# Sparse attention and a feed-forward layer on one core: value-row copies ahead of the weight loads, PSUM banks split by engine, plain bf16 transposes

## The chip, the cores and the metric

One core of a Trainium2 chip. In this kernel TensorE makes the matrix products, into buffers in the memory called PSUM (which is divided into banks); ScalarE, VectorE and GpSimd copy, reduce and cast, for the most part to and from the memory called SBUF; SyncE, and GpSimd for the weights, issue the transfers (DMA). A tile is a buffer that the kernel names. A timeline line gives start, length, engine and instruction, and in brackets how long the engine was idle before it and what ended that wait.

The metric is the time of one execution on the device, in microseconds (us). One profiled execution of each kernel gives the trace; its span is some 1.7 to 2.2 us shorter than the time. One of the four timed executions of the kernel before took 266.46 us and is left out of ratios as slow.

## The reference

Four batches, eight heads, 768 positions, head dimension 64. A query attends to the keys within 15 positions and to one maximum of keys (with the mean of values) for each block of 32. The result goes through a feed-forward layer.

```python
k_sum = k.reshape(B, H, nb, 32, D).max(axis=3)
v_sum = v.reshape(B, H, nb, 32, D).mean(axis=3)
scores = concat([where(|i - j| < 16, scale * q @ k.T, -1e9),
                 scale * q @ k_sum.T + log(32)])
attn = softmax(scores) @ concat([v, v_sum])
x = attn.transpose(0, 2, 1, 3).reshape(3072, 512)
h = x @ w_in                       # 512 -> 2048
out = (h * sigmoid(1.702 * h)) @ w_out   # 2048 -> 512
```

## The kernel before

The work goes in eight half units u0 to u7 of 384 tokens, two for each batch. A half unit is a first layer (16 tiles of four matmuls "ph") and a second layer (48 matmuls "po"). The attention of the next half unit is laid between the matmuls of the second layer. In the first layer of every odd half unit, the next batch's k and q are transposed on TensorE; I call this the preparation.

Tensors that the argument needs: kx holds transposed keys, with halo columns of the neighbours and 24 block maxima (ks) in every tile of 128 columns. qz holds transposed queries of two heads, with zeros in the half that belongs to the other head. vw holds values by tile; after v is cast into it, four copies move halo rows inside vw ("vw<-vw") and two copies bring in the block sums ("vw<-vs"); the function vrows casts the block sums (vs) on VectorE and has SyncE issue these six row copies. Only then can the first value product ("ps_av") run.

Keys are transposed by a product with the identity into an f32 PSUM tile of two banks. One engine copies them out, then VectorE takes maxima and halos:

```python
def tk_own(p, s, own):
    big = psb.tile([128, 1024], F32, name="ps_k", tag="big")
    for half in range(2):                       # one bank each
        p3 = big[:, half * 512:half * 512 + HALF].rearrange("p (c r) -> p r c", r=JH)
        for r in range(JH):
            pe.matmul(out=p3[:, r], lhsT=..., rhs=ident, start=True, stop=True)
    copy(own, at(flat, 0, ...), at(big, 0, ...))            # both banks at once
    return big

def tk_rest(p, s, big):
    dve.tensor_reduce(out=ks..., in_=at(big, 0, ...), axis=AX.X, op=ALU.max)
    ...                                         # three halo copies out of PSUM, one copy of ks
```

The start of the program, cut:

```python
for p in range(NP):
    clear_kx(dve, p, 0)
clear_vw(dve, 0)
dve.memset(vs[:, :, D:VC], float(block))
for p in range(NP):
    clear_qz(dve, p, 0)          # eight zeroings, while VectorE has no data yet
warmth(8)
...                              # k and v of batch 0: casts, tk_own, tk_rest, vsum
cast_q(dve, 0, 0)
cast_q(pool, 1, 0)
vrows(0)                         # vs cast on VectorE, six row copies issued by SyncE
for p in range(NP):
    load_q(0, p, 1)
tq(0, 0, act, dve, True)
...
cast_q(pool, 3, 0)
load_w_in(0)                     # weights at once; w_in 1..3 and w_out after the attention
scores(0, 0, 0)
...
```

The softmax here doesn't subtract the row's maximum and nothing guards it: scores larger than these inputs give would overflow.

Of the kernel before, what the change touches and what calls it, by code (L numbers as in the profile page):

```python
# [34 lines left out]
def kernel(  # L35
# [17 lines left out]
    QT = 64  # L53
# [18 lines left out]
    castp = ctx.enter_context(tc.tile_pool(name="cast", bufs=3))  # L72
# [10 lines left out]
    def load_k(b, p):  # L83
        t = stage.tile([128, 2, 2, JH, D], F32, name=f"kf{p}", tag=f"kf{p}")
        for half in range(2):
            sp.dma_start(out=t[:, half].rearrange("p h r d -> p h (r d)"),
                         in_=k[b, 2 * p:2 * p + 2, half * HALF:(half + 1) * HALF]
                         .rearrange("h (p r) d -> p h (r d)", r=JH))
        raw["k", p] = t

    def load_q(b, p, half):
        t = stage.tile([128, 2, JH, D], F32, name=f"qf{p}{half}", tag=f"qf{p}{half}")
        sp.dma_start(out=t.rearrange("p h r d -> p h (r d)"),
                     in_=q[b, 2 * p:2 * p + 2, half * HALF:(half + 1) * HALF]
                     .rearrange("h (p r) d -> p h (r d)", r=JH))
        raw["q", p, half] = t
# [39 lines left out]
    dve.memset(mk, 1.0)  # L136
# [13 lines left out]
    def finish_masks():  # L150
# [4 lines left out]
        for par, halo in ((0, 96), (1, 32)):  # L155
# [10 lines left out]
    qz = [[keep.tile([128, TH, 2, QT], BF16, name=f"qz{p}_{s}") for s in range(2)]  # L166
          for p in range(NP)]
# [14 lines left out]
    def clear_qz(eng, p, s):  # L182
        eng.memset(qz[p][s][0:64, :, 1, :], 0.0)
        eng.memset(qz[p][s][64:128, :, 0, :], 0.0)
# [24 lines left out]
    def cast_k(eng, p, eng2=None):  # L209
        t = castp.tile([128, 2, JH, 2, D], BF16, name="kb", tag="kb")  # L210
        for half in range(2):
            copy((eng2 or eng) if half else eng, t[:, half].rearrange("p r h d -> p h r d"), raw["k", p][:, half])
        cast["k", p] = t

    def cast_q(eng, p, half):
        t = castp.tile([128, JH, 2, D], BF16, name="qb", tag="qb")
        copy(eng, t.rearrange("p r h d -> p h r d"), raw["q", p, half])
        cast["q", p] = t
# [40 lines left out]
    def tk(p, s, own=dve):  # L259
        tk_rest(p, s, tk_own(p, s, own))  # L260

    def tk_own(p, s, own):
        src = cast.pop(("k", p))
        big = psb.tile([128, 1024], F32, name="ps_k", tag="big")
        for half in range(2):
            p3 = big[:, half * 512:half * 512 + HALF].rearrange("p (c r) -> p r c", r=JH)
            for r in range(JH):
                pe.matmul(out=p3[:, r], lhsT=src[:, half, r].rearrange("p h d -> p (h d)"),
                          rhs=ident, start=True, stop=True)

        flat = kx[p][s].rearrange("p t c -> p (t c)")
        copy(own, at(flat, 0, [[768, 2], [256, JH], [192, 2], [1, 64]]),
             at(big, 0, [[512, 2], [128, JH], [64, 2], [1, 64]]))
        return big

    def tk_rest(p, s, big):
        flat = kx[p][s].rearrange("p t c -> p (t c)")
        ks = attp.tile([128, nb], BF16, name="ks", tag="ks")
        dve.tensor_reduce(out=ks.rearrange("p (h n) -> p h n", h=2),
                          in_=at(big, 0, [[512, 2], [block, nb // 2], [1, block]]),  # L280
                          axis=AX.X, op=ALU.max)

        dve.tensor_copy(out=at(flat, 256 + 96, [[768, 2], [256, 2], [-176, 2], [1, 16]]),
                        in_=at(big, 128 - 16, [[512, 2], [128, 2], [16, 2], [1, 16]]))
        dve.tensor_copy(out=at(flat, 768 + 96, [[-176, 2], [1, 16]]),
                        in_=at(big, HALF - 16, [[512 - HALF + 16, 2], [1, 16]]))
        dve.tensor_copy(out=at(flat, 128 + 32, [[768, 2], [256, JH], [-48, 2], [1, 16]]),
                        in_=at(big, 64 - 16, [[512, 2], [128, JH], [16, 2], [1, 16]]))
        dve.tensor_copy(out=at(flat, 64, [[256, NJ], [64, 2], [1, nb]]),
                        in_=ks.unsqueeze(1).unsqueeze(1).to_broadcast([128, NJ, 2, nb]))  # L290

    def tq(p, half, e0, e1, early=False):
        src = cast.pop(("q", p))
        big = (pmm.tile([128, 512], F32, name="ps_q1", tag="mm") if early else
               psb.tile([128, 1024], F32, name="ps_q", tag="big"))
        ps = big[:, 0:HALF]
        p3 = ps.rearrange("p (c r) -> p r c", r=JH)
        for r in range(JH):
            pe.matmul(out=p3[:, r], lhsT=src[:, r].rearrange("p h d -> p (h d)"),
                      rhs=ident, start=True, stop=True)  # L300
        for hh, eng in ((0, e0), (1, e1)):
            r = slice(hh * 64, hh * 64 + 64)
            copy(eng, qz[p][half][r, :, hh, :], ps[r].rearrange("p (t c) -> p t c", c=QT))
# [3 lines left out]
    def scores(b, half, p):  # L307
        a_sb[p] = attp.tile([128, 2, TH, QT], BF16, name="a_sb", tag="a_sb")
        a = a_sb[p]
        big = psb.tile([128, 1024], F32, name="ps_s", tag="big")  # L310
        ps = big[:, 0:2 * HALF].rearrange("p (t h c) -> p t h c", h=2, c=QT)
        for i in range(TH):
            pe.matmul(out=ps[:, i].rearrange("p h c -> p (h c)"),
                      lhsT=kx[p][b % 2][:, half * TH + i, :],
                      rhs=qz[p][half][:, i].rearrange("p h c -> p (h c)"),
                      start=True, stop=True)
        act.activation(out=a.rearrange("p h t c -> p t h c"), in_=ps,
                       func=ACT.Exp, scale=scale)
        af = a.rearrange("p h t c -> p h (t c)")
        dve.tensor_mul(af, af, mk[:, half * TH:(half + 1) * TH, :]  # L320
                       .rearrange("p t c -> p (t c)").unsqueeze(1)
                       .to_broadcast([128, 2, TH * QT]))
# [64 lines left out]
    for p in range(NP):  # L387
        clear_qz(dve, p, 0)
    warmth(8)

    cast_k(act, 0, dve)
    big0 = tk_own(0, 0, act)
    cast_k(act, 1, dve)
    tk_rest(0, 0, big0)
    big1 = tk_own(1, 0, act)
    cast_k(pool, 2)
    tk_rest(1, 0, big1)
    cast_k(pool, 3)
    warmth(2)
    cast_v(act, 0, 0, 1)  # L400
    cast_v(pool, 0, 0, 0)
    big2 = tk_own(2, 0, act)
    vsum(0, (0,))
    cast_v(act, 0, 1, 1)
    cast_v(pool, 0, 1, 0)
    tk_rest(2, 0, big2)
    vsum(0, (1,))
    big3 = tk_own(3, 0, act)
    for j in (2, 3, 4, 5):
        cast_v(act, 0, j, 1)  # L410
        cast_v(pool, 0, j, 0)
        if j == 2:
            tk_rest(3, 0, big3)
            finish_masks()
        warmth(1)
        vsum(0, (j,))
    cast_q(dve, 0, 0)
    cast_q(pool, 1, 0)
    vrows(0)
    for p in range(NP):  # L420
        load_q(0, p, 1)
    tq(0, 0, act, dve, True)
    cast_q(dve, 2, 0)
    tq(1, 0, act, dve, True)
    cast_q(pool, 3, 0)
    load_w_in(0)
    scores(0, 0, 0)
    tq(2, 0, act, dve, True)
    scores(0, 0, 1)
    tq(3, 0, act, dve, True)  # L430
    scores(0, 0, 2)
    warmth(1)
    values(0, 0, 0)
    scores(0, 0, 3)
    warmth(1)
# [11 lines left out]
    for c in range(1, 4):  # L447
        load_w_in(c)
# [21 lines left out]
    for u in range(2 * B):  # L470
        b, half = u // 2, u % 2
        todo = {}
        if half == 0:

            for p in range(NP):
                cast_q(pool, p, 1)
                todo[3 + 3 * p] = [lambda p=p: tq(p, 1, dve, dve)]
                if p == 2:
                    todo[3 + 3 * p].append(lambda: None)
        elif b + 1 < B:  # L480
            s = (b + 1) % 2
            todo = {1: [lambda: tk(0, s)], 2: [lambda: tk(1, s)],
                    4: [lambda: vsum(s, (0, 1, 2))],
                    5: [lambda: vsum(s, (3, 4, 5)), lambda: vrows(s)],
                    6: [lambda: tk(2, s)], 8: [lambda: tk(3, s)],
                    9: [lambda: tq(0, 0, dve, dve)], 11: [lambda: tq(1, 0, dve, dve)],
                    12: [lambda: tq(2, 0, dve, dve)], 14: [lambda: tq(3, 0, dve, dve)]}
            cast_k(pool, 0)
            cast_k(pool, 1)
            for j in range(NJ):  # L490
                cast_v(pool, s, j, 0)
                cast_v(pool, s, j, 1)
            cast_k(pool, 2)
            cast_q(pool, 0, 0)
        for nt in range(NT):
            ff_in(u, nt)
            if half == 1 and b + 1 < B:
                if nt == 2:
                    cast_k(pool, 3)
                if nt == 9:  # L500
                    cast_q(pool, 1, 0)
                    cast_q(pool, 2, 0)
                if nt == 11:
                    cast_q(pool, 3, 0)
            for f in todo.get(nt, ()):
                f()
        if half == 0 and b + 1 < B:
            pass
# [4 lines left out]
        for ms, part in order:  # L513
# [4 lines left out]
            if half == 0 and b + 1 < B and i == 1:  # L518
                load_k(b + 1, 0)
                load_k(b + 1, 1)  # L520
                load_v(b + 1)
                load_k(b + 1, 2)
                load_k(b + 1, 3)
                for p in range(NP):
                    load_q(b + 1, p, 0)
                for p in range(NP):
                    load_q(b + 1, p, 1)
# [30 lines left out]
```

## Time and profile before

| kernel before | us |
|---|---|
| time, median of 3 | 260.46 (260.34 to 266.46) |
| span of the profile | 258.7 |
| first layer of u0 begins | 37.05 |
| first layer u0; u1, u3, u5 (with preparation); u2, u4, u6; u7 | 12.30; 16.87; 12.15; 10.84 |
| second layers u0 to u6 | 13.88 to 13.89 each |
| start of the last second layer to the end | 14.23 |

These lengths run from the start of one stage on TensorE to the start of the next, so they add up to the span. TensorE is the engine that sets them nearly everywhere.

### The profile page before, as it was taken

The numbers are of one execution on the slowest core, as the hardware profiler recorded it, in microseconds if no ns is written. First come the engines' busy times: TensorE is split into PE (matmuls) and PEld (weight loads), VectorE is DVE, ScalarE is ACT, GpSimd is POOL, SyncE is SP. The second block draws the span as 40 slices with busy tenths as digits, with TensorE's granted clock in tenths as the row PEclk, the third lists the DMA queues.
The fourth block names the chain that finished last, engine by engine and source line by source line (L and its number), as shares of the span: only waits on it lengthen the run. The fifth ranks groups of instructions, "written<-read, shape, count | busy, mean of one in ns | idle before, by whom it ended". The sixth has DMA issues, their size and how long they took to land.

```text
span 258.7 us, 4314 instructions
## 1 busy us (share of the span) xinstructions
PE 235.8 (91%) x1596; PEld 143.2 (55%) x1618; DVE 151.1 (58%) x357; ACT 132.7 (51%) x220; POOL 69.9 (27%) x157
## 2 busy tenths in 40 slices
PE   7555499999989999999989999999989999999994
PEld 2324356655656656566655656566655556565541
DVE  6876353377896745375995744386994825381000
ACT  2655147734547446844447356735447276727610
POOL 7649713085211007810220016902030000000000
PEclk9986589999999999999999999999999999999999
DMA  6999999999350139982140249961321110111012
GB/s 178 249 201 154 233 231 224 201 213 326 135 106 0 43 113 249 230 262 85 21 84 3 81 130 222 279 224 44 54 52 43 41 43 1 41 43 41 0 43 82
DMA packets 52982, 32.36 MB, mean 125 GB/s; under 512 B 26848, under 2 KB 49888, under 8 KB 52960
## 3 DMA queue, kind: packets, MB, share of 16 engines
q1 hardware_dynamic: 48736, 27.88, 41.5%
q0 software_dynamic: 4224, 4.19, 10.0%
q8 instruction: 13, 0.21, 0.4%
q14 instruction: 9, 0.07, 0.1%
HBM read 27.26 MB, written 6.29 MB: 130 GB/s over the span
## 4 chain that ended last, share of the span: by engine, by line
PE 75%; DVE 10%; DMA 5%; ACT 5%; SPq 2%; issue 1%; POOL 0%; ACTq 0%; DVEq 0%
PE po L27 29%; PE ph L27 25%; PE ps_av L27 5%; DVE kx L27 4%; PE ps_q L27 4%; PE ps_s L27 4%; PE ps_x L27 3%; DMA vw<-vs 3%; PE ps_k L27 3%; ACT L27 2%; DVE ks L27 2%; DMA vf<-in_v_dram 2%; SPq L27 2%; DVE x_sb L27 2%; PE ps_vs L27 2%
## 5 line engine op out<-in xcount | busy, mean ns | idle before, releaser
L27 PE MATMUL ph<-xT,w_in_sb 128*128 128x384 bf16 x512 | 95.5, 329 | 0.9 <-ACT gT L27 0.8
L27 PE MATMUL po<-w_out_sb,gT 128*128 128x512 bf16 x363 | 92.5, 379 | 0.8
L27 ACT ACTIVATE gT<-ph 128x384 bf16<-128x384 f32 x128 | 61.4, 491 | 39.5 <-PE ph L27 38.7
L27 PEld LDWEIGHTS <-w_in_sb 128*128 128x128 bf16 x512 | 51.8, 104 | 30.4 <-issue 3.6
L27 PEld LDWEIGHTS <-gT 128*128 128x128 bf16 x384 | 34.6, 97 | 28.0
L27 DVE CAST qz<-ps_q 64x384 bf16<-64x384 f32 x60 | 33.3, 555 | 28.4 <-PE ps_q L27 26.8
L27 POOL CAST qb<-qf 128x384 bf16<-128x384 f32 x30 | 15.2, 512 | 97.4 <-PE ps_q L27 69.2
L27 ACT ACTIVATE a_sb<-ps_s 128x768 bf16<-128x768 f32 x32 | 25.2, 810 | 27.5 <-PE ps_s L27 27.3
L27 DVE TENSOR_TENSOR x_sb<-ps_av,rc 64x384 bf16<-64x384 f32 x64 | 35.5, 555 | 1.5
L27 DVE TENSOR_TENSOR a_sb<-a_sb,mk 128x768 bf16<-128x768 bf16 x32 | 19.1, 599 | 28.2 <-ACT a_sb L27 27.2
L27 ACT ACTIVATE osb<-po 128x512 f32<-128x512 f32 x24 | 14.3, 597 | 41.1 <-PE ps_x L27 23.3
L27 POOL CAST vw<-vf 128x512 bf16<-128x512 f32 x42 | 25.2, 639 | 12.3 <-DMA vf<-in_v_dram 12.2
L27 DVE CAST kx<-ps_k 128x128 bf16<-128x128 f32 (+3 forms) x60 | 21.7, 405 | 5.7 <-PE ps_k L27 5.7
L27 POOL CAST kb<-kf 128x384 bf16<-128x384 f32 x28 | 14.7, 544 | 29.8 <-PE ps_k L27 24.4
L27 PE MATMUL ps_av<-vw,a_sb 128*128 128x130 bf16 x192 | 17.2, 228 | 5.8 <-DMA vw<-vs 5.4
L27 PEld LDWEIGHTS <-a_sb 128*128 128x128 bf16 x192 | 14.1, 101 | 13.1 <-issue 5.5
L27 ACT ACT_TABLE_LOAD x16 | 20.5, 1283 | 1.1 <-PEq L542 0.8
L27 PE MATMUL ps_q<-ident,qb 128*128 128x128 bf16 x96 | 16.9, 323 | 3.4 <-DVE kx L27 2.2
L27 PE MATMUL ps_s<-qz,kx 128*128 128x128 bf16 x192 | 17.3, 231 | 0.7 <-DVE qz L27 0.7
L27 PEld LDWEIGHTS <-kx 128*128 128x128 bf16 x192 | 14.5, 106 | 6.2 <-issue 1.2
L27 DVE TENSOR_REDUCE ks<-ps_k 128x24 bf16<-128x768 f32 x16 | 15.2, 949 | 1.7 <-ACT kx L27 1.6
L27 PEld LDWEIGHTS <-qb 128*128 128x128 bf16 x96 | 9.8, 120 | 10.0 <-issue 3.2
(45 smaller groups left out, 124.9 us busy)
## 6 DMA issues: line engine op xcount, KB each, us to landing
kf<-in_k_dram SPq DMA_DIRECT2D x32, 192.0 KB, 3.5
vf<-in_v_dram SPq DMA_DIRECT2D x24, 256.0 KB, 5.0
qf<-in_q_dram SPq DMA_DIRECT2D x32, 192.0 KB, 4.6
out_dram<-osb SPq DMA_DIRECT2D x24, 256.0 KB, 2.0
w_in_sb<-in_moe_w_in_dram POOLq DMA_DIRECT2D x4, 512.0 KB, 12.2
w_out_sb<-in_moe_w_out_dram POOLq DMA_DIRECT2D x4, 512.0 KB, 24.8
vw<-vs SPq DMA_DIRECT2D x8, 148.5 KB
vw<-vw SPq DMA_DIRECT2D x8, 99.0 KB, 2.8
```

Of the source, the lines that this page charges most:

```text
L27: r = f(*a, **kw)
```

## The change

Three intents. The copies of value rows get the DMA engines for themselves, with the weights waiting behind them (the "gate") and the next batch's loads waiting for the first layer's end (the "hold"). In the first unit ScalarE and VectorE read different PSUM banks at the same time. In batches 1 to 3, k and q are transposed by real transposes into dense bf16 PSUM. The core of the diff:

```diff
-    for p in range(NP):
-        clear_qz(dve, p, 0)
     warmth(8)
 ... in the start, between the key transposes and the block sums:
+    clear_qz(dve, 0, 0)
+    clear_qz(dve, 1, 0)
     ks3 = tk0(3)
+        if j == 3:
+            clear_qz(dve, 2, 0)
+            clear_qz(dve, 3, 0)
 ... tk0, for batch 0: same matmuls into the same tile "big", then
+        for half in range(2):
+            act.activation(out=at(flat_kx(p, 0), 768 * half, ...),
+                           in_=at(big, 512 * half, ...), func=ACT.Copy)
+            o = 1 - half
+            dve.tensor_reduce(out=ks[:, o * 12:o * 12 + 12],
+                              in_=at(big, 512 * o, ...), axis=AX.X, op=ALU.max)
 ... tq0, for batch 0: the q transposes are made twice, one tile for each engine
 ... the gate; the weights follow on the same queue:
+    pool.tensor_copy(out=gate[0:nb, :], in_=vw[0][0:nb, 1, 0, 0:2])
+    pool.tensor_copy(out=gate[64:64 + nb, :], in_=vw[0][64:64 + nb, 0, 0, 0:2])
+    for c in range(4):
+        load_w_in(c)
 ... the hold, before the loads of batch 1:
+                if b == 0:
+                    sp.dma_start(out=hold, in_=gT[0][0:16, NT - 1, 0:16])
 ... batches 1 to 3:
+    def trans(src):
+        big = psb.tile([128, 2048], BF16, name="ps_t", tag="big")
+        for j in range(NJ):
+            pe.transpose(out=big[:, j * 128:(j + 1) * 128], in_=src[:, j], identity=ident)
+        return big[:, 0:S]
+    def tk(p, s):
+        ps = trans(...)
+        dve.tensor_copy(out=at(flat_kx(p, s), 0, ...), in_=ps...)
+        dve.tensor_reduce(out=ks, in_=ps..., axis=AX.X, op=ALU.max)
+        key_halos(p, s)          # three copies, now from SBUF
+        key_rows(p, s, ks)
 ... all of q in the preparation; k and q of batches 1 to 3 loaded in 256 B runs;
     u0's late q transposes from tile 6 on instead of tile 3
```

## The prediction

> **What bounds the kernel now.** I read the page first, then the chain of waits, the busy times of each stage, the groups by form, and the timeline of one feed-forward stage.
>
> ```profile
> PE 235.8 (91%) x1596; PEld 143.2 (55%) x1618; DVE 151.1 (58%) x357; ACT 132.7 (51%) x220; POOL 69.9 (27%) x157
> ...
> PEclk9986589999999999999999999999999999999999
> DMA  6999999999350139982140249961321110111012
> ```
>
> TensorE is busy 91%. Its clock drops only in slices 3 to 6 (one slice is 6.47 us), so the start is a stage apart. The DMA engines are full there, up to slice 9.
>
> The chain of waits in the first 40 us (start, length, what):
>
> ```profile
> 20.36 0.35 SPq L27
> 20.71 0.05 issue
> 20.76 8.12 DMA vw<-vs
> 28.87 0.14 issue
> 29.01 0.82 PE ps_av L27 x6
> ```
>
> The first value product cannot begin before the rows of block sums have been copied into vw. That copy takes 8.12 us, and the waits say that TensorE idles 5.37 us for it. The timeline has the four w_in loads issued from 19.31 and the four w_out loads from 22.38, so the copy shares the DMA engines with 8.4 MB of weights.
>
> Busy time by stage (start:end, length, then engines; clock, DMA share and GB/s last). The first two stretches are one half unit without preparation of a batch, the third is one with it:
>
> ```profile
> 94.00:106.50 12.50, 12.34 (x80) 7.75 (x79) 4.80 (x9) 9.12 (x18) 6.91 (x13) 1.00 0.95 219
> 106.50:120.00 13.50, 13.20 (x105) 7.85 (x106) 8.99 (x19) 5.97 (x9) 4.11 (x8) 1.00 0.67 207
> 120.00:136.90 16.90, 16.14 (x109) 10.58 (x108) 14.61 (x33) 9.11 (x17) 3.75 (x8) 1.00 0.26 56
> ```
>
> 12.5 us is first layer plus q transposes, 13.5 us second layer plus attention of the next half. 16.9 us is first layer plus all k transposes, the block sums and half of the q transposes; there VectorE is busy 14.61 of 16.9 us, and TensorE has gaps.
>
> **What the operations cost.** The groups by form:
>
> ```profile
> L27 DVE CAST qz<-ps_q 64x384 bf16<-64x384 f32 x60 | 33.3, 555 | 28.4 <-PE ps_q L27 26.8 <-ACT qz L27 0.8
> ...
> L27 DVE CAST kx<-ps_k 128x768 bf16<-128x768 f32 x12 | 11.4, 953 | 5.7 <-PE ps_k L27 5.7
> ...
> L27 DVE COPY xT<-ps_x 128x384 bf16<-128x384 bf16 x28 | 10.0, 358 | 3.6 <-PE ps_x L27 2.9
> ```
>
> And TensorE's timeline, where the old transposes (ps_q) stand beside the real transposes (ps_x):
>
> ```profile
> 97.03 0.49 PE L27 MATMUL ps_q<-ident,qb 128*128 128x128 bf16 x3
> 97.32 2.15 PE L27 MATMUL ph<-xT,w_in_sb 128*128 128x384 bf16 x12
> 99.31 0.49 PE L27 MATMUL ps_q<-ident,qb 128*128 128x128 bf16 x3
> ...
> 113.88 0.33 PE L27 MATMUL ps_x<-ident,x_sb 128*128 128x128 bf16 x3
> 114.05 0.50 PE L27 MATMUL ps_s<-qz,kx 128*128 128x128 bf16 x6
> ```
>
> The starts tell the price, not the lengths. From 97.03 to 99.31 are 2.28 us for three q transposes and twelve ph of 0.1625 us (1.95), so 0.33 for three: 0.11 us each. Three ps_x take 114.05 - 113.88 = 0.17, so 0.057 us each. The difference: ps_q is a product with the identity into f32 PSUM at every third column; ps_x is a transpose into dense bf16.
>
> **What the Trainium skill says.** "PSUM — Partial Sum Buffer", Specifications (TRN2), lists 8-byte cachelines and says that a non-contiguous access pattern slows matmuls significantly: the 0.11 against 0.057 us agrees. "VectorE: DVE Perf Modes", The perf-mode tier table, has tensor_copy from PSUM at up to 2x and tensor_reduce at 1x always. The trace agrees with the first: f32 costs (953 - 555)/384 = 1.04 ns per column with 0.156 us fixed, and 358 ns for 384 bf16 columns is 0.53 ns per column with the same fixed part. The reduction (949 ns over f32) should therefore gain nothing from bf16; no bf16 one is in this trace. "DMA: Bandwidth & Descriptors", Specifications, asks for 512 B for line rate: here v, in 256 B runs, moved 216 to 236 GB/s in 8 to 14 us, and k and q, in 768 B runs, up to 338. "TensorE: Matmul & The Clock Gate", Part 1, has the clock halve after an idle window of about 3.4 us; here it fell to 0.50 at 27 to 28 us, within the idle stretch, and came back at 34.
>
> **The change, part by part.**
>
> *Value rows first.* The weights are now gated behind the landing of the rows. SyncE issued the six row copies from 16.94 to 21.56, after the last block-sum product, and that stays. Without other traffic the same six, in the later batch, went from the first issue at 70.05 to the end of the DMA activity at about 76.3, 6.3 us. So they should land at 16.94 + 6.3 = 23.2, with some q loads beside them say 24. The other path to the first value product is TensorE's: 12 more q transposes at half clock (12 x 0.16 = 1.9 us), less the two one-after-the-other evacuations of about 0.5 us that the split banks save, after scores that ended at 23.6 before: about 24.4. That sets it: 29.0 becomes 24.4, 4.6 us. With no idle stretch the clock should be full from about 24 on rather than from 34, and two fillers go; the 8.0 us from there to the first layer (37.05) lose perhaps 0.8, as VectorE's four 1.4 us normalisations keep most. First layer: 37.05 to about 31.7, gain 5.4.
>
> *The price of it: late weights.* All weights took 414 us of engine time (10.0% of 16 x 258.7), at the observed share of 1.0 to 1.2 that is 21.6 to 26 us, 2.7 to 3.2 per piece of eight. Issued from about 24.5, with 2 us latency and the late q loads beside them, w_in lands at about 30, 33, 36 and 39. The first layer needs one piece every 2.6 us from 31.7: 31.7, 34.3, 36.9, 39.8. This is on the edge; I charge 0.8 us. w_out's pieces at 42 to 52 precede their needs at 43.5 to 54. Net gain of the start: 4.6.
>
> *Banks by engine.* tk0 has ScalarE and VectorE read different banks at once. The start of vrows hangs on v's arrival (last cast ends 16.45), so this gives nothing of its own.
>
> *Plain transposes.* In each half unit with preparation, 36 transposes of 0.11 (3.96 us) become 48 of 0.057 (2.74), as all of q moves there. TensorE needs 16 x 0.65 = 10.4 + 2.74 + 6 x 0.216 = 14.4 us, where it took 16.9. VectorE per k pair: the copy 953 becomes 0.156 + 768 x 0.53 = 0.56, the reduction stays at 0.95, the three halo copies (346 + 179 + 279 = 0.80) come from SBUF at about 0.2 each, the row copy stays at 0.22; the start-to-start 2.57 becomes about 1.95. Four are 7.8; q is 8 x 0.56 = 4.5 for the whole batch; vs 0.68; sum 13.0 against 14.6, and PSUM is free after copy and reduction alone. Following the order, the last q copy ends about 0.6 us after the last ph, and scores 3 needs it only later, so TensorE should not wait: 2.5 us gained, three times: 7.5. The half units without preparation lose 12 x 0.11 = 1.3 us each, in units 2, 4 and 6: 3.9. Unit 0 keeps its old transposes.
>
> *Smaller runs.* k and q of batches 1 to 3 now come in 256 B runs. 4.7 MB at 220 GB/s are 21.4 us, where 24 us pass between the first load and the preparation: hidden for batches 2 and 3. Batch 1's loads are held back to about 43.5 and share with w_out until 52; q3 then lands at 69 to 71, and its transposes are wanted at about 71. I charge 0.7.
>
> Sum: 4.6 + 7.5 + 3.9 - 0.7 = 15.3 us off the span of 258.7, so 243.4; the time was 1.7 above the span (260.36 against 258.7), so 245.1.
>
> **Rivals.** (1) The weights become the bound of the first unit: each us that the rows land later moves all eight pieces. For it: the edge above and a DMA share of 1.2 in 24 to 52. Against it: next batch's loads, which shared that stretch, are held away. It costs up to 3 us: 248. (2) VectorE bounds the preparation in place of TensorE, if the halo copies of 16 columns or the two-byte reads from PSUM are slower than worked out: it has 1.4 us to spare in 14.4. If nothing runs at 2x, k costs 9.4 and q 7.7, and the stage stays at about 17: then 7.5 goes, and the time is near 252. Against it: the 358 ns of xT. (3) vrows now comes four tiles later, and the next values wait for its copies again. The block sums end at about 9.2 us of the stage, landing is 6.3 later, 15.5; values start at 18.5: 3 us to spare. If it fails, about 1 us per batch: 248. (4) The weights were hiding nothing, and TensorE's first scores set 29 anyway: its scores were done at 23.6, so no.
>
> **Range.** Terms: start 3 to 6, preparation 4.5 to 8.5, plain half units 3.5 to 4.2, late loads 0 to 2. Unlikely to be all low at once: 240.5 to 249.5. Slower by 2% would need all gains gone and a new wait; within 2% (above 255.3) would need the start and the preparation to fail together. Faster 0.96, same 0.03, slower 0.01.
>
> **What would show it.** The row copy off the chain or at 3 us or less; values from about 24.4 and the first layer from 31 to 32.5; no wait of ph for w_in over 1 us; ps_k and ps_q of later batches at 0.057 us start to start; kx copies near 0.56 us and reductions still near 0.95; preparation stages of about 14.4, plain first layers of about 11.2 us; the second layers unchanged at 13.5 to 13.9. Wrong if TensorE waits on weights for several us, or if the preparation stage stays above 16.

## The result, and the profile after

| | before | after |
|---|---|---|
| time, median | 260.4 (4 runs) | 250.97 (4 runs, 250.07 to 251.37) |
| ratio | | 0.964, 95% interval 0.9604 to 0.9675 |
| span | 258.7 | 248.8 |
| first layer of u0 begins | 37.05 | 36.43 |
| first layer u0 | 12.30 | 12.26 |
| first layers u1, u3, u5 | 16.87 each | 15.35, 14.49, 14.50 |
| first layers u2, u4, u6 | 12.15 each | 10.84, 10.84, 10.85 |
| sum of the seven second layers | 97.22 | 97.42 |
| last second layer to the end | 14.23 | 14.98 |

A ratio is the mean time of one kernel's fast runs over that of the other's of the same rounds, so it is not quite the ratio of the medians quoted.

The kernel is faster by 9.5 us, not by 15.3. It lies outside the predicted range. The spans split the 9.9 us between them: start 0.62, preparations 1.52 + 2.38 + 2.37 = 6.27, plain first layers 3.93, less 0.2 in the second layers and 0.75 at the end.

The page of the kernel after, busy times and slices (columns as in the prediction):

```profile
PE 229.8 (92%) x1628; PEld 137.4 (55%) x1628; DVE 129.5 (52%) x336; ACT 132.7 (53%) x224; POOL 67.6 (27%) x136
...
PEclk9866899999999999999999999999999999999999
DMA  6984799999995119999032249995051110111011
```

VectorE lost 21.6 us of busy time and TensorE 6.0. A slice is now 6.22 us. The clock's dip is now in slices 2 to 5 (0.8, 0.6, 0.6 and 0.8), where it was in 3 to 6. The DMA share falls in slices 3 to 5, as the weights now wait; the first layer begins in slice 6 as before.

The groups by form show what the transposes cost now (operation, output<-input, count, busy us and ns of one, idle before):

```profile
L27 DVE COPY qz<-ps_t 64x768 bf16<-64x768 bf16 x24 | 13.3, 555 | 2.3 <-PE ps_t L27 1.9
L27 DVE TENSOR_REDUCE ks<-ps_t 128x24 bf16<-128x768 bf16 x12 | 11.3, 946 | 0.0
...
L27 DVE COPY kx<-ps_t 128x768 bf16<-128x768 bf16 x12 | 6.6, 551 | 4.2 <-PE ps_t L27 4.2
...
L27 DVE COPY kx<-kx 128x80 bf16<-128x80 bf16 x32 | 4.7, 187 | 0.1
```

A copy of 768 bf16 columns takes 551 ns where 768 f32 columns took 953, and the maximum takes 946 where it took 949. Both are as predicted. TensorE's timeline gives the price of one transpose:

```profile
64.04 0.50 PE L27 MATMUL ps_t<-ident,kb 128*128 128x128 bf16 x6
64.38 0.81 PE L27 MATMUL ph<-xT,w_in_sb 128*128 128x384 bf16 x4
```

Six transposes from start to start take 0.34 us, 0.057 each. Busy time by stage (start:end, length, PE, PEld, DVE, ACT, POOL; clock, DMA share, GB/s) of the first preparation, a plain first layer and the second preparation:

```profile
62.62:77.97 15.35, 14.66 (x121) 9.46 (x119) 12.98 (x33) 8.96 (x17) 8.99 (x14) 1.00 1.05 226
91.86:102.70 10.84, 10.68 (x68) 6.25 (x65) 0.36 (x1) 8.93 (x17) 3.18 (x4) 1.00 1.11 207
...
116.75:131.24 14.49, 14.49 (x121) 9.52 (x119) 11.89 (x33) 8.96 (x17) 0.78 (x1) 1.00 0.26 56
```

TensorE has no gap left in the second preparation: 14.49 busy of 14.49. In the first TensorE misses 0.69 us, while GpSimd is busy for 8.99 us and VectorE for 1.1 us more than in the second.

So the middle of the program did what was worked out. The start did not. The chain of waits of the kernel after, in its start:

```profile
15.35 0.69 DVE kx L27 x4
16.04 0.20 DVE qz L27
...
22.08 0.22 DVE qz L27
22.30 0.03 issue
22.33 0.69 DVE vs L27
23.02 0.28 DVE qb L27
23.30 0.05 issue
23.34 1.46 PE ps_q L27 x6
```

VectorE's zeroings of qz are on the chain, four from 16.04 and four from 21.21. In the kernel before they ran at 2.90 to 5.2, before there was data. The copy of the block sums ("vs") begins at 22.33; before it began at 17.83. And the scores wait for a cast of q that stands behind that copy: TensorE idles 5.08 us before 23.34. Its granted clock is 0.50 from 22 to 26 us in this trace and full again from 28.

The timeline of the first key pair shows a second loss, first in the kernel before and then in the kernel after (start, length, engine, instruction; idle before and its releaser):

```profile
6.50 0.81 ACT L27 ACTIVATE kx<-ps_k 128x768 bf16<-128x768 f32 x1 [2.60 <-PE ps_k L27]
...
7.35 0.96 DVE L27 TENSOR_REDUCE ks<-ps_k 128x24 bf16<-128x768 f32 x1 [0.73 <-ACT kx L27]
```

```profile
6.18 0.49 ACT L27 ACTIVATE kx<-ps_k 128x384 bf16<-128x384 f32 x1 [2.25 <-PE ps_k L27]
6.70 0.56 DVE L27 TENSOR_REDUCE ks<-ps_k 128x12 bf16<-128x384 f32 x1 [2.35 <-ACT kx L27]
7.29 0.49 ACT L27 ACTIVATE kx<-ps_k 128x384 bf16<-128x384 f32 x1 [0.63 <-DVE ks L27]
...
7.82 0.56 DVE L27 TENSOR_REDUCE ks<-ps_k 128x12 bf16<-128x384 f32 x1 [0.56 <-ACT kx L27]
```

The two engines were meant to work side by side. They take turns: copy, maximum, copy, maximum, from 6.18 to 8.38, 2.20 us, where one copy and one maximum of both banks took 6.50 to 8.31, 1.81 us. Two smaller instructions cost more than one large one (two copies of 0.49 us against one of 0.81, two maxima of 0.56 against one of 0.96), and ScalarE now waits for VectorE in the middle. ScalarE's last value casts end at 20.31 instead of 16.43, and SyncE issues the first row copy at 19.82 instead of 16.94.

The two losses together used up most of what the gate gave. The rows still landed earlier: GpSimd's gate got them at 27.50, and the first value product began at 28.19 instead of 29.01.

```profile
27.50 0.41 POOL L27 COPY gate<-vw 24x2 bf16<-24x2 bf16 x2 [8.63 <-DMA vw<-vs]
...
28.19 0.51 PE L27 MATMUL ps_av<-vw,a_sb 128*128 128x130 bf16 x6
```

### The profile page after: what moved, and what is told of

It reads as the page before. It is cut to its first block, busy times and chain, and to the rows that moved or that the text cites. A ratio compares the mean times of both kernels' runs of the same rounds, so it can differ in the third digit from the quotient of the medians.

```text
span 248.8 us, 4320 instructions
## 1 busy us (share of the span) xinstructions
PE 229.8 (92%) x1628; PEld 137.4 (55%) x1628; DVE 129.5 (52%) x336; ACT 132.7 (53%) x224; POOL 67.6 (27%) x136
## 4 chain that ended last, share of the span: by engine, by line
PE 76%; DVE 11%; ACT 6%; DMA 2%; SPq 1%; issue 1%; POOL 0%; ACTq 0%; DVEq 0%
PE po L27 31%; PE ph L27 29%; PE ps_s L27 4%; PE ps_av L27 4%; DVE x_sb L27 3%; PE ps_t L27 3%; ACT L27 3%; DMA vf<-in_v_dram 2%; PE ps_vs L27 2%; PE ps_x L27 2%; DVE kx L27 2%; PE ps_q L27 2%; DVE ks L27 2%; SPq L27 1%; DVE a_sb L27 1%; ACT osb L27 1%
## 5 line engine op out<-in xcount | busy, mean ns | idle before, releaser
L27 PE MATMUL po<-w_out_sb,gT 128*128 128x512 bf16 x384 | 95.6, 379 | 0.0
L27 PE MATMUL ph<-xT,w_in_sb 128*128 128x384 bf16 x512 | 91.8, 326 | 0.9 <-ACT gT L27 0.8
L27 PEld LDWEIGHTS <-w_in_sb 128*128 128x128 bf16 x512 | 48.8, 98 | 32.0 <-issue 3.6
L27 POOL CAST kb<-kf 128x768 bf16<-128x768 f32 (+1 forms) x16 | 12.5, 785 | 78.9 <-DMA kf<-in_k_dram 76.9
L27 POOL CAST vw<-vf 128x512 bf16<-128x512 f32 x42 | 26.3, 663 | 4.7 <-DMA vf<-in_v_dram 4.6
L27 POOL CAST qb<-qf 128x768 bf16<-128x768 f32 (+1 forms) x19 | 13.6, 722 | 8.5 <-DMA qf<-in_q_dram 7.0
L27 DVE COPY qz<-ps_t 64x768 bf16<-64x768 bf16 x24 | 13.3, 555 | 2.3 <-PE ps_t L27 1.9
L27 PEld LDWEIGHTS <-kb 128*128 128x128 bf16 x96 | 8.9, 119 | 8.3 <-ACT kb L27 2.9
L27 PEld LDWEIGHTS <-x_sb 128*128 128x128 bf16 x96 | 7.8, 97 | 10.0 <-DVE x_sb L27 2.3
L27 DVE CAST qz<-ps_q 64x384 bf16<-64x384 f32 x12 | 6.7, 557 | 10.5 <-PE ps_q L27 10.3
```

The source lines that it names most:

```text
L27: r = f(*a, **kw)
```

## The experiments

Fifteen kernels ran, all with correct results, in the order below; every kernel of one call shared the runs of the kernel before on one chip. The kernel after ran in a call of its own, where the kernel before had 260.4; in the four calls below it had 259.59, 260.08, 259.83 and 259.87. Between calls, ratios are therefore the safer comparison. Stage lengths come from one profile of each kernel. Letters in the recorded expectations are labels of the theories that a call weighs; the text after each says in words which reading the numbers support. "Row copies" is SyncE's first issue of vw<-vw, "vs" the copy of the block sums, "values" the first ps_av, "first layer" the first ph of u0, all in us from the span's start. Twelve kernels ran with 3 rounds, the last three with 5.

| kernel | row copies | vs | values | first layer | u0 | first prep. | time | ratio |
|---|---|---|---|---|---|---|---|---|
| before | 16.94 | 17.83 | 29.01 | 37.05 | 12.30 | 16.87 | 260.4 | 1 |
| after | 19.82 | 22.33 | 28.19 | 36.43 | 12.26 | 15.35 | 250.97 | 0.964 |
| e1 zeroings early | 18.32 | 20.65 | 26.36 | 34.60 | | | 249.71 | 0.9608 |
| e2 two tiles | 17.46 | 20.67 | 26.20 | 34.43 | | | 248.88 | 0.958 |
| e3 both | 17.10 | 18.76 | 24.49 | 32.73 | 11.68 | 15.54 | 246.84 | 0.950 |
| b3 transposes alone | 16.98 | 17.90 | 29.07 | 37.10 | 12.26 | 14.85 | 249.84 | 0.9609 |
| b4 old start, gate, hold, transposes | 16.69 | 17.58 | 23.98 | 32.32 | 11.85 | 15.29 | 245.72 | 0.9464 |
| d3 b4 with another hold | 16.74 | 17.63 | 23.91 | 31.50 | 11.89 | 15.04 | 245.46 | 0.9445 |

### First call: which part of the start lost the gain

My theory: the turns of the two engines and the moved zeroings together delay the value rows. The rival: the rows were bound elsewhere (the values were limited by the scores, or the gate was worth little), so mending either would move nothing.

**e1_clear_early**: the zeroings go back to the idle start.

```diff
     dve.memset(vs[:, :, D:VC], float(block))
+    for p in range(NP):
+        clear_qz(dve, p, 0)
     warmth(8)
...
-    clear_qz(dve, 0, 0)
-    clear_qz(dve, 1, 0)
...
-        if j == 3:
-            clear_qz(dve, 2, 0)
-            clear_qz(dve, 3, 0)
```

> The changed kernel with the eight zeroings of qz put back to the start of the program, where VectorE idles. In the changed kernel they take about 2.2 us of VectorE between the key reductions and the copy of the block sums (16.0 to 17.1 and 21.2 to 22.3), and the first layer began at 36.43 instead of the predicted 31.7. Theory O (order on VectorE's queue: work was moved ahead of the sums): the sums are copied at about 20.2 instead of 22.3, the first layer begins at about 34.3, the time falls by about 2 us to 249. Theory P (the two engines take turns on the key banks, which holds ScalarE's value casts): the first row copy stays near 19.8 and the time falls by less than 1 us.

Measured: 249.71 (248.51 to 250.52), ratio 0.9608 (0.9571 to 0.9646). The values came 1.83 us earlier than in the kernel after, and the first layer 1.83. The interval overlaps that of the kernel after, so the time alone does not settle it. The trace does, for the first reading (the order on VectorE's queue): vs was copied at 20.65, where it had 20.2, and the first layer began at 34.60, where it had 34.3. The row copies came earlier too, at 18.32: in the kernel after, the zeroings also held ScalarE, which waits 1.58 us for VectorE's maximum before its copy at 17.75.

**e2_two_tiles**: each bank gets a PSUM tile of its own. The instructions, their shapes and their order on each engine stay; the second bank now comes from another pool of buffers.

```diff
-        big = psb.tile([128, 1024], F32, name="ps_k", tag="big")
+        bigs = [psb.tile([128, 1024], F32, name="ps_k", tag="big"),
+                pmm.tile([128, 512], F32, name="ps_k1", tag="mm")]
...
-                           in_=at(big, 512 * half, ...),
+                           in_=at(bigs[half], 0, ...),
...
-                              in_=at(big, 512 * o, ...),
+                              in_=at(bigs[o], 0, ...),
```

> The changed kernel with the two halves of each key transpose of batch 0 in two PSUM tiles instead of one tile of two banks, so that ScalarE and VectorE need not wait for each other on the first half. Theory P: evacuations of one key pair take about 1.1 us instead of 2.2; ScalarE's value casts end near 16.5 instead of 20.3, the first row copy goes out near 17 instead of 19.8, the sums are copied near 19.5, the first layer begins near 33.5: time about 248. Theory O: VectorE's own work is unchanged in length, so the sums are copied at most 1 us earlier, and the time stays within 1 us of 250.9.

Measured: 248.88 (248.30 to 249.42), ratio 0.958 (0.9552 to 0.9608). The timeline of its first key pair:

```profile
4.97 0.49 ACT L27 ACTIVATE kx<-ps_k 128x384 bf16<-128x384 f32 x1 [0.97 <-PE ps_k L27]
5.29 1.02 DVE L27 TENSOR_REDUCE ks<-ps_k 128x12 bf16<-128x384 f32 x2 [0.94 <-PE ps_k L27]
5.89 0.49 ACT L27 ACTIVATE kx<-ps_k 128x384 bf16<-128x384 f32 x1 [0.43 <-DVE ks L27]
```

VectorE begins 0.32 us after ScalarE, before ScalarE's copy is done, and what released it is TensorE and no longer ScalarE. The pair of copies and maxima ends 1.41 us after the first start (ScalarE's second copy ran 5.89 to 6.38), instead of 2.20; 1.1 had been expected, but ScalarE still waits 0.43 us for VectorE to leave the second bank. The first copy also starts earlier, at 4.97 instead of 6.18: in the kernel after it began only when all six transposes of the pair were done. So the turns came from sharing one tile: the wait was put in for the tile, not for the bank. "PSUM — Partial Sum Buffer" of the Trainium skill, PSUM bank collisions raise a hardware error, says that accesses of two engines to different banks run clean at the same time; this run agrees, with correct results and 0.17 us of overlap between the first copy and the first maximum. The chip allowed the split. The way the kernel described its buffers did not. The row copies left at 17.46 (17 expected), vs was copied at 20.67 (19.5) and the first layer began at 34.43 (33.5): right in direction, and short of the sizes, as the zeroings still stood in the queue.

**e3_two_tiles_clear**: both edits at once.

> Both edits at once. If both causes count and add: first row copy near 17, sums near 17.5 to 18, rows landed near 24, values from about 24.4, first layer from about 32: time 246 to 247. If they are one and the same cause, no better than the better of the two alone. If neither, about 250.9, and the start is bound by something else, such as VectorE's chain from the first mask product to the last normalisation (28.2 to 36.2 in the changed kernel).

Measured: 246.84 (246.43 to 247.08), ratio 0.950 (0.9475 to 0.9525). The two edits take 0.0032 and 0.0060 off the ratio one at a time and 0.0140 together, 0.8, 1.6 and 3.6 us of 260. The surplus of the ratio lies within the intervals; in the traces the two losses simply add. The first layer begins 1.83, 2.00 and 3.70 us earlier than in the kernel after, and the spans are 2.0, 2.1 and 4.1 us shorter. Neither edit does the other's work: with the turns gone, the zeroings still hold vs to 20.67; with the zeroings gone, the row copies still leave at 18.32. With both mended the values begin at 24.49, where the prediction had 24.4. Now the first layer waits for the weights:

```profile
32.73 2.45 PE L27 MATMUL ph<-xT,w_in_sb 128*128 128x384 bf16 x14 [1.04 <-DMA w_in_sb<-in_moe_w_in_dram]
```

1.04 us, where the prediction had charged 0.8. That charge was right in kind. In the kernel after, whose first layer begins 3.7 us later, no such wait shows.

**e4_ungated**: the two gate copies are taken out, so that the weights leave at once.

```diff
-    gate = consts.tile([128, 2], BF16, name="gate")
     hold = consts.tile([16, 16], BF16, name="hold")
-    pool.tensor_copy(out=gate[0:nb, :], in_=vw[0][0:nb, 1, 0, 0:2])
-    pool.tensor_copy(out=gate[64:64 + nb, :], in_=vw[0][64:64 + nb, 0, 0, 0:2])
```

> The changed kernel without the two small copies that hold the weights back until the value rows have landed; the eight weight loads then go out from about 19. If the gate is worth what it was meant for, the row copies, issued from 19.8 to 24.8, share with the weights and land 8 us after the last issue, near 33, the first layer begins near 41, and the time is about 255 to 256. If the gate is worth nothing (the start is set by TensorE's and VectorE's chain alone), the time stays within 1 us of 250.9.

Measured: 254.73 (254.54 to 254.81), ratio 0.9803 (0.9776 to 0.9831). TensorE waits 3.50 us for the block sums, and the first layer begins at 41.00.

```profile
32.71 0.81 PE L27 MATMUL ps_av<-vw,a_sb 128*128 128x130 bf16 x6 [3.50 <-DMA vw<-vs]
```

So the gate was worth 4.6 us at the first layer, 3.8 in the span and in the time (4.2 by ratio), in the very kernel whose start seemed to have gained nothing. The rival falls.

### Second call: the parts alone, from the side of the kernel before

**b1_gate_before**: the kernel before with the gate and nothing else.

```diff
     cast_q(pool, 3, 0)
-    load_w_in(0)
+    gate = consts.tile([128, 2], BF16, name="gate")
+    pool.tensor_copy(out=gate[0:nb, :], in_=vw[0][0:nb, 1, 0, 0:2])
+    pool.tensor_copy(out=gate[64:64 + nb, :], in_=vw[0][64:64 + nb, 0, 0, 0:2])
+    for c in range(4):
+        load_w_in(c)
...
-    for c in range(1, 4):
-        load_w_in(c)
```

> The kernel before with one part of the change alone: all eight weight loads wait for the landing of the value rows; the next batch's loads are not held back. Theory G (the row copies' 8 us were the DMA engines' sharing with the weights): rows land near 24 instead of 28.9, values from about 24.2. Theory W (the weights then come too late, as the next batch's k and v loads share with them): w_in's last piece lands 17 us after its issue at 27.5, near 44.5, where it is needed near 41, so TensorE waits about 3 to 4 us in the first layer and the time falls by only 1 to 2 us, to 258. If W is wrong, the time falls by 4.6 us to 255.

Measured: 259.02 (258.05 to 259.47), ratio 0.996 (0.9935 to 0.9985). The values begin at 24.20, 4.8 us earlier, as the prediction had it for the gate. But the first layer begins at 33.87 and waits for w_in first (2.47 us), u0's first layer takes 13.45 instead of 12.30 and its second layer 14.74 instead of 13.88. Most of the gain is given back further down, where the next batch's loads run beside the late weights.

**b2_gate_hold_before**: the hold is added.

```diff
+                if b == 0:
+                    sp.dma_start(out=hold, in_=gT[0][0:16, NT - 1, 0:16])
                 load_k(b + 1, 0)
```

> The same with the next batch's loads held back until the first layer of unit 0 is done. Theory W: the weights now come in time but for up to 1 us, and the time falls by 4 to 4.6 us, to about 255.2. If the hold makes batch 1's preparation late, up to 1 us of that goes.

Measured: 257.5 (257.35 to 257.64), ratio 0.9907 (0.989 to 0.9924); I had expected 255.2 and missed. The first layer begins at 31.68, 5.4 us earlier than before. But u0's first layer takes 13.86. The late q transposes still come after tile 3, and TensorE waits 1.39 us at 36.42 for GpSimd's cast of q, which starts at 35.86. With an earlier first layer, the transposes have to come later. The change moves them to tile 6, which in the diff looks like tidying; in b4, which has this too, the same cast starts at 35.88, the first of these transposes at 37.05, and the first layer takes 11.85. No run moved the transposes alone. And the end of the span is 14.94 long instead of 14.23 (more below).

**b3_plain_only**: the kernel after with before's start, no gate and no hold, so the transposes alone (with the new order and sizes of the later loads, and u0's late q transposes from tile 6 on). **b4_gate_plain**: the same with gate and hold and no other difference. Both, against the kernel after:

```diff
+    for p in range(NP):
+        clear_qz(dve, p, 0)
     warmth(8)
-    ks0 = tk0(0)
+    big0 = tk_own(0, 0, act)
...                          # the start in the order of the kernel before, through vrows(0)
-    tq0(0, 0)
+    tq_b0(0, 0, act, dve, True)      # each q pair transposed once, as before
...
     gate and hold: in b4 only
```

> The changed kernel with the start of the kernel before (key evacuation by whole tile, zeroing at the start, weights not held, next batch's loads not held): the plain transposes of batches 1 to 3 alone. By the stage lengths in the two traces, preparation 16.87 to 14.5 (three times) and plain first layers 12.15 to 10.84 (three times) should give 11.0 us: 248.7. If the 256 B loads or the late start of the next batch make the first preparation late, as in the changed kernel (15.35), 249.5. If the gain of the changed kernel came partly from its start, less: 252.

> The start of the kernel before with the gate and the hold, and the plain transposes: the change without the bank split, without the moved zeroings and without the doubled q transposes. If the start parts and the transposes add: 259.6 less 4.4 less 10.2, about 245.0, where the prediction of the change was 245.1; values from about 24.2, the first layer near 32.5. If the split had a value of its own beyond its tile's turn-taking, this is slower than the split with two tiles and early zeroing (246.8).

b3 measured: 249.84 (248.94 to 250.47), ratio 0.9609 (0.9583 to 0.9636). The whole change (0.964) is worth no more than its transposes. b4 measured: 245.72 (245.48 to 247.01), ratio 0.9464 (0.9437 to 0.9491). This is the change without its bank split, its moved zeroings and its double q transposes, and it lands near what I had predicted for the whole (245.1). The double q transposes were never run alone: e3 has them and b4 does not, and the intervals of the two overlap. Its timeline in the start:

```profile
17.58 0.68 DVE L27 CAST vs<-ps_vs 128x512 bf16<-128x512 f32 x1
...
23.98 0.81 PE L27 MATMUL ps_av<-vw,a_sb 128*128 128x130 bf16 x6 [0.91 <-ACT a_sb L27]
...
32.32 2.95 PE L27 MATMUL ph<-xT,w_in_sb 128*128 128x384 bf16 x16 [0.24 <-DMA w_in_sb<-in_moe_w_in_dram]
```

The first value product waits for the scores (ScalarE), as the prediction said it would once the rows were early. Its gain by stages is start 4.73, u0 0.45, preparations 1.58 + 2.38 + 2.37, plain first layers 3.93, less some 0.2 in the second layers and 0.7 at the end: 14.5 of a span that is 14.6 shorter.

### Third call: attempts at a better start

b4 and e3 still wait for w_in or are close to it. The second half of u0's q loads stands beside the weights, so I moved it ahead.

**c1_qearly_b4** (b4 with it) and **c2_qearly_e3** (e3 with it):

```diff
-    for p in range(NP):
-        load_q(0, p, 0)
+    for half in range(2):
+        for p in range(NP):
+            load_q(0, p, half)
...
     vrows(0)
-    for p in range(NP):
-        load_q(0, p, 1)
```

> The start of the kernel before with gate, hold and plain transposes (245.7), with the four loads of q's second half issued before the value rows instead of after them. Theory: after the gate w_in's first piece landed 7.5 us after its issue because those q loads (issued 21.3 to 23.5) share with it; without them it lands about 5.5 us after and the first layer does not wait (0.24 us before); gain 0.2 to 0.5 us: 245.3. Rival: the rows now queue behind the q loads and land later than 24; then 246 or more.

> The changed kernel with two PSUM tiles and early zeroing (246.8), with the same move of q's loads. TensorE waited 1.04 us for w_in's first piece there; if the q loads are why it is late, that wait goes and the time falls by about 0.5 to 1.0 us, to 246.0; if the piece is late for its own 512 KB, the wait stays.

c1: 246.81 (246.01 to 247.12), ratio 0.9492. c2: 247.05 (246.51 to 248.22), ratio 0.9512. The wait for w_in went, and the first layers began 0.3 and 0.7 us earlier (32.03 and 32.07), but u0's first layer grew by as much (12.26 in both). First layer plus start is 44.3 in c1 where it was 44.2 in b4, and 44.3 in c2 where it was 44.4 in e3. The wait at the front was exchanged for waits further on, and neither run showed the gain expected (245.3 and 246.0).

**c3_masks**: c2 with the masks made in three parts, the later two after the first scores are under way, so that VectorE reaches vs sooner.

```diff
-            finish_masks()
+            masks_a()
...
     tq0(1, 0)
+    masks_b()
...
     tx(3, act)
+    masks_c()
```

> The kernel of the run before, with the masks in three parts, so that VectorE copies the block sums and casts q 1 before the mask copies it does not yet need. TensorE idled 1.79 us for that cast. If VectorE's queue bounds the start, q's second transposes begin at about 18.2 instead of 19.8, values near 23.5, the first layer near 31 if the weights allow; gain up to 1 us over the run before: 245.2. If the rows' landing (24.4) or the weights bound it, nothing.

Measured: 247.18 (245.83 to 247.47), ratio 0.950. vs was copied at 19.16 where c2 had 19.37, q's second transposes began at 20.30 instead of 20.38 (18.2 expected), and the first layer began at 33.24 instead of 32.07. Taking this work out of VectorE's queue hardly brought vs forward, and the expected 245.2 was missed.

**c4_rows_act**: c3 with the two vs copies issued by ScalarE's queue, beside the four on SyncE's.

```diff
-        sp.dma_start(out=w5[64:64 + nb, :, 0], ...
+        (two or sp).dma_start(out=w5[64:64 + nb, :, 0], ...
...
-    vrows(0)
+    vrows(0, act)
```

> The kernel of the run before, with the two copies of the block sums issued by ScalarE beside SyncE's four, so that the six row copies are issued in about 2.8 us instead of 4.6. If the rows' landing bounds the start and the weights behind it, rows land near 22 to 22.5, the weights start 2 us earlier and the first layer is no longer held by them: 1 us or more over the run before, 244.2. If ScalarE's 1.8 us of issuing delays its exponentials as much, nothing or a loss.

Measured: 248.53 (247.82 to 249.43), ratio 0.9574: slower than c3. SyncE's four issues took 3.96 us instead of 2.76, ScalarE's two took 2.28 where SyncE's two had taken 1.88, and the gate got the rows at 25.66 instead of 24.45, where 22 to 22.5 had been expected. The last issue did end earlier (21.29 instead of 22.00), so what took longer was the way from issue to landing.

### Fourth call: the first preparation and the end

What stayed open was why the first preparation takes 14.85 to 15.6 us where the later ones take 14.5, and why the end is 0.75 us longer.

**d1_hold_mid**: b4 with the hold released by an earlier tile of the first layer, so that batch 1's loads leave earlier.

```diff
-                    sp.dma_start(out=hold, in_=gT[0][0:16, NT - 1, 0:16])
+                    sp.dma_start(out=hold, in_=gT[0][0:16, 11, 0:16])
```

> The start of the kernel before with gate, hold and plain transposes (245.7), the hold let go when tile 11 of the first layer of unit 0 is done instead of tile 15. Theory L (batch 1's loads come late): the first preparation falls from 15.29 to at most 14.9, the time by about 0.4 us, as long as w_out, which lands by 48 for needs from 44.2 on, is not delayed enough to be waited for. Rival: the first preparation is long because GpSimd's casts run beside VectorE's small copies in it; letting go 2.6 us earlier shifts the casts and shows the same 15.3, or w_out is late and the second layer grows above 13.93.

Measured: 245.78 (245.70 to 246.18), ratio 0.9461 (0.9438 to 0.9484). The first preparation took 15.43, no less than b4's 15.29; at most 14.9 had been expected.

**d2_hold_dve** and **d3_hold_dve_mid**: the same waits made by a small VectorE copy into the buffer that the first load overwrites, with no DMA of its own; d2 waits for the last tile, d3 for tile 11.

```diff
         t = stage.tile([128, 2, 2, JH, D], F32, name=f"kf{p}", tag=f"kf{p}")
+        if b == 1 and p == 0:
+            dve.tensor_copy(out=t[0:16, 0, 0, 0, 0:16], in_=gT[0][0:16, NT - 1, 0:16])   # d3: 11
...
-                    sp.dma_start(out=hold, in_=gT[0][0:16, NT - 1, 0:16])
```

> The same kernel (245.7) with the hold made by one small VectorE copy into the tile that the first held load fills, so no extra DMA on SyncE's queue. Theory D (the extra DMA shifts the last stores): the end after the issue of the last store is 2.9 to 3.0 us again instead of 3.7, and the time falls by 0.7 to 0.8 us to 245.0. Rival: the end differs by chance from build to build or with the gate, and stays at 3.7.

> Both: hold by VectorE, let go at tile 11. If L and D are right and add, 1.1 us below 245.7: 244.6, below the prediction of the change.

d2: 245.58 (245.12 to 245.89), ratio 0.9448 (0.942 to 0.9475). d3: 245.46 (244.64 to 245.58), ratio 0.9445 (0.9419 to 0.947). d3 is the best that I ran. It clearly beats both kernels, by 14.4 us against the kernel before (medians) and some 5 us against the kernel after (0.9445 against 0.964), but not b4, d1 or d2: their intervals overlap. The first preparation took 15.63 in d2 and 15.04 in d3, so with this hold an earlier release went with a shorter stage, which b4 and d1 don't show. One profile of each does not settle what late loads cost.

The end (last second layer's start to the end of the span) is 14.11 to 14.23 in the three kernels without a hold (before, b1, b3), 14.8 to 15.0 in those with gate and hold DMA (b2 and b4 among them), 14.63 in e4 (hold, no gate), and 14.47 in d2 and d3. In all of them TensorE and ScalarE do the same in this stretch (the last copy out of PSUM starts 10.6 us into it); the difference comes after the last store's issue, 2.9 to 3.0 us without a hold, 3.4 to 3.8 with its DMA, 3.24 in d2 and d3. Taking the hold's DMA away brought back 0.45 of it in the trace of d2 (14.92 in b4, 14.47); the times of the two are not apart. Where the rest comes from stays open.

For the first preparation, the timeline of the kernel after:

```profile
61.01 7.14 POOL L27 CAST vw<-vf 128x512 bf16<-128x512 f32 x12 [0.31 <-DMA vf<-in_v_dram]
...
66.03 1.06 DVE L27 COPY kx<-kx 128x80 bf16<-128x80 bf16 x3
...
68.93 0.36 DVE L27 COPY kx<-kx 128x80 bf16<-128x80 bf16 x3
```

Three halo copies take 1.06 us while GpSimd casts v, and 0.36 after it is done; the copy of ks takes 0.67 and then 0.22. TensorE then waits 0.69 us at 69.15 for VectorE to free PSUM. The same stretch shows in b4, e3, d1 and d3 with 0.5 to 1.15 us. "SBUF — State Buffer" of the Trainium skill, Who interferes with whom, has VectorE's fast copies share a pair of ports with GpSimd, one of them blocked for the whole instruction of the other; the stretched copies agree with that. The copies out of PSUM stay at 0.54 to 0.56. In the second preparation GpSimd is busy 0.78 us, and it took 14.49. The nearest thing to a test is b3: without the hold the loads come earlier, GpSimd is busy 4.46 us in its first preparation instead of 8.99, and the stage takes 14.85. Its excess over the later ones is 0.36 us instead of 0.86. But the DMA share falls with it, from 1.05 to 0.85, and in e3, d1 and d2 TensorE also waits 0.23 to 0.37 us there for a late cast of q. No run took GpSimd's casts away and left all else, so GpSimd's part is an association that the traces show, and not a cause that a run has shown.

## Why the prediction was wrong

**The failed step: banks by engine.** "The start of vrows hangs on v's arrival (last cast ends 16.45), so this gives nothing of its own." The row copies hang on v's arrival only as long as ScalarE is free when v arrives. The split gave the engines no parallel work, since one tile holds both banks, and made ScalarE wait for VectorE. ScalarE's value casts ended at 20.31. "SyncE issued the six row copies from 16.94 to 21.56, after the last block-sum product, and that stays" fell with it: they were issued from 19.82, and the last two from 23.05. e2 shows it by its one edit: the row copies left at 17.46 and the first layer began 2.00 us earlier.

**Its companion, which the prediction never priced:** eight zeroings went from VectorE's idle start into the middle of its queue. They take 1.11 us for each four, and both fours lie on the chain. Mending them alone (e1) was worth 1.83 us at the first layer. I had read the diff for operations added and removed; these had the same number and size, only another place. e1 and e3 show what they cost.

**The term start, 4.6 predicted, 0.62 measured.** The mechanism was right. The gate is worth 3.8 us of time (e4 against after; 4.2 by ratio), gate and hold together 4.1 (b4 against b3, 245.72 against 249.84). With both faults mended the values begin at 24.49 and with the old start at 23.98, for 24.4 predicted; the start gains 4.32 and 4.73. Part of this is luck: the prediction got to 24.4 with twelve more q transposes at half clock, where b4 has none more and e3 makes them at full clock (1.00 from 16 to 34 us). And the way from there to the first layer, 8.0 us, was to lose 0.8; less the wait for weights it took 7.20 in e3, but 8.10 in b4, whose clock was 0.50 from 20 to 28. The charge of 0.8 for late weights was 1.04 in e3, 0.24 in b4. The prediction counted on the hold against late weights, but did not see how much hangs on it and on the later q transposes: the gate alone gives 1.0 us and gate with hold 2.4 in the kernel before (b1 and b2, by ratio).

**Preparations, 7.5 predicted, 6.27 measured.** 2.5 each was 2.38 and 2.37 in the second and third; the durations of copy, maximum and transpose were right to within 0.01 us. The first gained only 1.52. I had charged late loads 0.7 of their own; what came is 0.86 in this stage (15.35 against 14.49). That the size fits may be luck: 0.69 of it is a wait for VectorE's small copies, stretched while GpSimd casts. Late loads put those casts there, and which of the two counts no run separates (b3, d1 to d3).

**Plain first layers, 3.9 predicted, 3.93 measured.** Right, as 12 transposes of 0.11 less. The length of about 11.2 us that the prediction named as a sign was too long: it took off 1.3 from 12.5, a stretch with rounded ends, where the stage measured 12.15; it is now 10.84.

**The end, 0 predicted, 0.75 lost,** and 0.2 in the second layers. Nothing in the prediction looked there; some 0.45 of it goes with the hold's DMA, and the rest is open.

The terms add up: 15.3 - 4.0 (start) - 1.2 (preparations) + 0.7 (late loads, counted there) - 0.95 (end and second layers) = 9.85, for 9.9 measured. The rivals I listed concerned the weights, VectorE in the preparation, the rows of later batches and TensorE's first scores. None of them concerned the order of VectorE's and ScalarE's work in the first 22 us, where the range of the start (3 to 6) was too narrow for a part that I had set to zero without tracing its waits.

## What to carry to other kernels

When a change splits a buffer between engines, look at what unit the waits are put in for: two banks in one tile are one buffer for the scheduler, and the split then costs two turns in place of one; give each engine its own tile. Price moved instructions as well as added ones: a zeroing that was free in an idle start costs its full length in the middle of a queue that others wait for. And test a change of several parts by part, since here one part (the gate) gave some 4 us of which two others took back 3.7 at the first layer, and the total looked like the transposes alone.

## What the Trainium skill lacked or had wrong

- "PSUM — Partial Sum Buffer", PSUM bank collisions raise a hardware error, says that different banks can be read at once, which the runs confirm. It does not warn that a kernel that keeps two banks in one tile gets waits between engines for the tile: 2.20 us in turns, 1.41 in two tiles.
- "SBUF — State Buffer", Who interferes with whom, gives no size for small copies beside GpSimd's casts. Here three copies of 80 columns went from 0.36 us to as much as 1.15, and one of 288 columns from 0.22 to as much as 0.86 (the traces show them beside each other; no run isolated it).
- "DMA: Bandwidth & Descriptors", Rules for kernel authors, says of spreading issues over several engines that it saves issue time only. With two queues issuing row copies at once, SyncE's four issues took 3.96 us instead of 2.76 and ScalarE's two 2.28 where SyncE's had taken 1.88, and the rows were there 1.2 us later, though the last issue ended 0.7 us earlier.
- The lengthening of the end has no explanation in the pages consulted: 14.1 to 14.2 us without a hold, 14.8 to 15.0 with gate and hold DMA, 14.47 with a hold on VectorE. Its cause is open.
